# A chunked recurrence with attention behind it: scans and a transpose put behind a mask in VectorE's order

## The chip, the cores and the metric

The kernel runs on one core of a Trainium2 chip. The metric is the device time of one execution in microseconds; the median of several runs is compared. A core has five engines with an instruction queue each: TensorE (PE in the profile), VectorE (DVE), ScalarE (ACT), GpSimd (POOL) and SyncE (SP), which here issues the DMAs. Each takes its instructions in the order in which the program issues them and waits for the others by semaphores.

## The reference

Two stages. The first is a recurrence with a matrix state for each of 4 x 8 heads, over 768 time steps, with 40 x 40 numbers in a state:

```
for t in range(768):
    y[t]  = r[t] @ state
    Sa    = state @ a[t]
    state = state * w[t] - outer(Sa, b[t]) + outer(v[t], k[t])
```

The second takes y as x (4 batches, 768 rows, 320 columns) and computes four attention experts with a causal softmax, of which each row gets its two best by a gate, weighted:

```
for e in range(4):
    ye   = softmax(causal((x @ wq[e]) @ (x @ wk[e]).T / 8)) @ (x @ wv[e]) @ wo[e]
    out += gate[:, e] * ye
```

## The kernel before

The time axis is cut into 24 chunks of 32 steps (NC), and four chunks make a group W of 128 steps (NW = 6 groups). Inside a chunk the recurrence becomes products of small matrices, and the state is handed from chunk to chunk. The work falls into a loop by chunk and a preparation by group.

The loop (MAIN, line 387) runs n from 0 to 24. A step n has ten slots, 0 to 9, and each issues one piece: 0 g of chunk n (products of the state, line 328), 1 f of chunk n-1 (line 342) with its **mask** FX on VectorE (line 343; "F's mask"), 2 t of chunk n-1, 3 u of chunk n (line 333), 4 y of chunk n-1 (lines 353 and 355, 64 products that read FX), 5 z of chunk n-1 (XT, line 357, VectorE), 6 the keys of chunk n+1, 7 s of chunk n (line 373) with the **state update** ST on VectorE (line 380; at a group's last chunk with a gauge, line 364), 8 w of chunk n, 9 v of chunk n+1. The next g reads ST.

The preparation of group W is put into the slots of the steps before it. It is written as strings in SIDE: row r, which holds for step n = 4(W-1) + r, is split at "/", and the k-th part is issued behind the piece of slot k. The first group is prepared in START, and for W=1 rows 0 to 3 come from SIDE1. The letters that the change touches, with a digit ahead of it for one of the two halves of the heads (0 or 1):

- a: suffix products by a scan (line 192, VectorE); b: a reciprocal and a copy (lines 194, 195, VectorE); s: a second scan (line 197, VectorE), which needs a and b.
- X: products with the result of s, two instructions (line 201, GpSimd); K and H: products with the result of a, two instructions each (line 205, GpSimd). Below, the four of K and H of a half are "K pieces", counted from 0K on.
- e: a load; f and g: two range checks (line 189, ScalarE).
- m0, m1: 64 products of a half on TensorE (line 226), for which X, K and H of that half must be done; then the masking of the result (line 229) and its transpose (line 231) on VectorE, and two masked copies on GpSimd (line 233).
- L: the **turning** of the masked products, one transpose of 128 x 1024 (line 242, VectorE), and two clearings (lines 243, 244, GpSimd).
- t and a number: so many of 28 **row operations** (lines 250 and 252, VectorE, in pairs) that invert triangular matrices; the first pair is the shortest and the last too, the middle ones are the longest.
- T: two transposes of the inverse (lines 257, 259, VectorE); B, D: copies on ScalarE (line 265); P, Q: 128 products each (line 272).

Every piece keeps the order of issue of its engine, so a scan in slot 8 stands on VectorE ahead of F's mask of the next step, and a scan in slot 1 behind it.

Of the kernel before, what the change touches and what calls it, by code (L numbers as in the profile page):

```python
# [25 lines left out]
    -3: "//l1///0w///1w",  # L26
    -2: "//l2/////l30f0g/0a0b0s",
    -1: "0X0K0H/1a1b/1e/////1K1H/1f1g1s1X",
    0: "///m0//////m1L",
    1: "/t16//B/////t12",  # L30
    2: "/T////////P",
    3: "///D//////Q",
}

# [1 line left out]
         (1, "0e0l0u1l1u1w1e"), (0, "o0"), (1, "0a0b0K0H"), (0, "i1 L B k0 x3 j47 t28 j0 j23 S o1 Z"), (1, "0f0g1f1g"), (0, "D"), (1, "0s1a0X1H"),  # L36
         (0, "P v0 Q"), (1, "1b1s"))

SIDE1 = ("////////n01p1xi0o0", "///n1i1o1L//Bt6//t8", "/t8//t6////T", "//P/D/////Q")


def layouts(r, k, v, w, a, b):
# [40 lines left out]
def recurrence(tc, ctx, I, xT, FL, CM, early, tail=None):  # L83
# [4 lines left out]
    V, A, T, PL, SY = nc.vector, nc.scalar, nc.tensor, nc.gpsimd, nc.sync  # L88
# [300 lines left out]
    def at(n, s, *fs):  # L389
        jobs.setdefault((n, s), []).extend(fs)  # L390

    def items(W, line, inv, td):

        fs, i = [], 0
        while i < len(line):
            x = line[i]
            if x == " ":
                i += 1
            elif x in "LTSZPQBD":
                fs.append(inv[x])  # L400
                i += 1
            elif x in "tj":
                j = i + 1
                while j < len(line) and line[j].isdigit():
                    j += 1
                m = int(line[i + 1:j])
                if x == "t":
                    fs += td[:m]
                    del td[:m]
                else:  # L410
                    fs.append(lambda m=m: busy(m))
                i = j
            else:
                y = line[i + 1]
                if x == "x":
                    fs.append(lambda y=y: fill(int(y)))
                elif x == "l":
                    fs.append(lambda y=y: load_k(W, int(y)))
                elif x == "c":
                    fs += [lambda k=k, y=y: load_c(int(y), k) for k in (range(4) if y == '0' else (1,))]  # L420
                elif x == "m":
                    fs.append(lambda y=y: mm(W, int(y)))
                elif x in "nio":
                    fs.append(lambda x=x, y=y: mm(W, int(y), x))
                elif x == "v":
                    fs.append(lambda y=y: units[int(y)]["v"]())
                elif x == "k":
                    fs.append(lambda y=y: keys(int(y)))
                else:
                    fs.append(preps[W, int(x)][y])  # L430
                i += 2
        return fs

    preps = {(w, a): prep(w, a) for w in range(NW) for a in range(2)}
    for W in range(1, NW):
        inv = invert(W)
        td = list(inv["t"])
        for r, line in SIDE.items():
            n = 4 * (W - 1) + r
            line = SIDE1[r] if W == 1 and r >= 0 else line  # L440
            for k, part in enumerate(line.split("/") if n >= 0 else ""):
                assert k < 10
                at(n, k, *items(W, part, inv, td))
        assert not td
# [406 lines left out]
def body(tc, I, out):  # L851
    with ExitStack() as ctx:
        dp = ctx.enter_context(tc.tile_pool(name="xd", bufs=1, space=DRAM))
        xT = dp.tile([4, 320, 768], F32, name="xT")
        fp = ctx.enter_context(tc.tile_pool(name="flag", bufs=1))
        FL = fp.tile([128, 24], F32, name="FL")
        CM = fp.tile([128, 261], F32, name="CM")
        FI = fp.tile([1, 1], I32, name="FI")
        with ExitStack() as c1:
            c1.enter_context(tc.manual_schedule())  # L860
            pre = []
            def tail(raw):
                p, jobs = prepare(tc.nc, ctx.enter_context(tc.tile_pool(name="pre", bufs=1, side="right", reuse_waits="tile")), I, xT, raw)
                pre.append(p)
                return jobs
            recurrence(tc, c1, I, xT, FL, CM, ExitStack(), tail)
        with ExitStack() as c2:
            moe(tc, c2, I, xT, out, CM[:, 0:128], pre[0], FL, FI)

        far = tc.nc.values_load(FI, min_val=0, max_val=1)  # L870
        with tc.If(far != 0):
            with ExitStack() as c3:
                c3.enter_context(tc.manual_schedule())
                step_by_step(tc, c3, I["RAW"], xT)
            with ExitStack() as c4:
                moe(tc, c4, I, xT, out, CM[:, 0:128], pre[0])
# [25 lines left out]
```

## Time and profile before

| | |
|---|---|
| runs, us | 609.68, 608.61, 610.55; median 609.68 |
| profiled execution, us | 608.79, its span 607.0 |
| mean granted TensorE clock | 0.986 of full speed |
| busy share of the span | PE 93%, DVE 78%, ACT 60%, POOL 42% |
| chain of work that ended last | PE 60%, DVE 22%, DMA 6%, ACT 5%, issue 3%, POOL 2% |

The chain is followed back from the last instruction of the execution to whatever released each step. Its shares tell which engines set the end over the whole span; what a change in one stretch is worth is read from that stretch.

### The profile page before, as it was taken

How to read it: one execution, taken by the hardware profiler on the slowest of the kernel's cores; microseconds unless marked ns; L12 is line 12 of the kernel's file. 1: busy time of each engine (PE TensorE's matmuls, PEld its weight loads, DVE VectorE, ACT ScalarE, POOL GpSimd, SP SyncE). 2: the span in 40 equal slices, each digit the busy share in tenths (PEclk: the TensorE clock that was granted, in tenths of full speed). 3: DMA queues.
4: the chain of work that ended last, by engine and by line, in shares of the span. 5: the costliest groups of instructions: out<-in, count | busy, mean ns of one | idle time of the engine just before them, and what ended most of it. 6: DMA issues, size and time to landing. Idle time of an engine off the chain costs nothing.

```text
span 607.0 us, 23642 instructions
## 1 busy us (share of the span) xinstructions
PE 566.0 (93%) x10111; PEld 496.1 (82%) x10111; DVE 475.9 (78%) x963; ACT 364.2 (60%) x740; POOL 257.3 (42%) x233
## 2 busy tenths in 40 slices
PE   7998999899999999999999879989999989999996
PEld 3547898899989989989999768878888878987884
DVE  8999899589498678766324369999989997898892
ACT  4854356367356456644546337757776777778873
POOL 5247309807914931960000232546544353333550
PEclk9999999999999999999999879989999999999998
DMA  6622352453354255223146244212311312020102
GB/s 153 176 89 57 119 150 69 119 143 117 94 162 123 78 145 148 67 71 97 49 138 159 55 115 117 53 50 68 84 43 45 82 36 70 24 53 11 56 2 72
DMA packets 44196, 54.09 MB, mean 89 GB/s; under 512 B 20098, under 2 KB 33666, under 8 KB 44082
## 3 DMA queue, kind: packets, MB, share of 16 engines
q1 hardware_dynamic: 43794, 52.32, 31.0%
q8 instruction: 82, 1.34, 0.9%
q10 hardware_dynamic: 288, 0.17, 0.2%
q14 instruction: 32, 0.26, 0.1%
HBM read 38.31 MB, written 7.86 MB: 76 GB/s over the span
## 4 chain that ended last, share of the span: by engine, by line
PE 60%; DVE 22%; DMA 6%; ACT 5%; issue 3%; POOL 2%; SPq 0%; DVEq 0%; ACTq 0%
PE pt L659 6%; PE ot L784 4%; PE pk L272 4%; PE sc L739 4%; PE ps L373 4%; PE pf L353 4%; PE pt L769 4%; PE pt L795 4%; PE pf L355 3%; PE pk L226 3%; PE pg L324 3%; PE pu L333 3%; PE pk L310 3%; PE pg L328 3%; PE pf L342 2%
## 5 line engine op out<-in xcount | busy, mean ns | idle before, releaser
L761 POOL TENSOR_TENSOR P<-P,m 128x128 f32<-128x128 f32 (+2 forms) x96 | 89.1, 950 | 116.5 <-DVE m L757 59.5
L201 POOL TENSOR_TENSOR AB<-EA,SC 40x1024 f32<-40x1024 f32 x18 | 48.9, 2714 | 83.5 <-PE pg L328 61.6
L750 ACT ACTIVATE P<-sc,m 128x128 f32<-128x128 f32 (+2 forms) x96 | 60.8, 634 | 25.5 <-DVE m L749 15.0
L784 PE MATMUL ot<-pt,vv 128*128 128x256 f32 (+1 forms) x384 | 61.1, 292 | 5.7 <-DVE ots L790 5.5
L739 PE MATMUL sc<-ks,qs 128*128 128x384 f32 (+4 forms) x256 | 62.3, 346 | 3.6 <-ACT P L750 2.9
L773 DVE TENSOR_TENSOR pt<-pt,pt 128x384 fp32r<-128x384 f32 (+1 forms) x96 | 59.0, 619 | 5.3 <-ACT pt L772 3.6
L784 PEld LDWEIGHTS ot<-pt,vv 128*128 128x128 f32 x384 | 51.5, 191 | 9.8 <-DVE ots L790 8.2
L749 DVE TENSOR_REDUCE m<-sc 128x1 f32<-128x128 f32 (+2 forms) x96 | 58.7, 615 | 0.9 <-PE sc L742 0.4
L772 ACT ACTIVATE pt<-pt 128x384 fp32r<-128x384 f32 (+1 forms) x96 | 51.9, 543 | 10.5 <-PE pt L769 9.0
L205 POOL TENSOR_TENSOR KB<-KB,SUF 104x512 f32<-104x512 f32 x38 | 57.0, 1534 | 0.9 <-DMA KB<-in_EK 0.5
L769 PE MATMUL pt<-CM,P 128*128 128x128 f32 x336 | 53.0, 275 | 3.8 <-DVE qs L668 2.6
L353 PE MATMUL pf<-FX,LS 128*40 128x64 f32 x768 | 47.7, 224 | 3.6 <-DVE FX L343 3.4
L353 PEld LDWEIGHTS pf<-FX,LS 128*40 128x40 f32 x768 | 42.3, 118 | 6.6 <-DVE FX L343 5.5
L659 PE MATMUL pt<-xh,wq 128*128 128x384 f32 x192 | 42.9, 359 | 4.7 <-DVE qs L668 4.5
L739 PEld LDWEIGHTS sc<-ks,qs 128*128 128x128 f32 x256 | 40.4, 191 | 7.4 <-ACT P L750 6.9
L355 PE MATMUL pf<-RX,SD 80*40 80x64 f32 x736 | 45.8, 222 | 0.0
L233 POOL TENSOR_TENSOR GK<-GK,CM 128x512 f32<-128x512 f32 x23 | 27.5, 1196 | 41.0 <-DVE GK L231 29.8
L335 ACT ACTIVATE R<-pu 32x640 f32<-32x640 f32 x48 | 33.3, 694 | 19.1 <-PE pu L333 18.5
L330 ACT ACTIVATE GT<-pg,CM 128x320 f32<-128x320 f32 x48 | 22.7, 523 | 36.3 <-PE pg L328 36.1
L343 DVE TENSOR_TENSOR FX<-pf,MK 128x1024 f32<-128x1024 f32 x24 | 29.1, 1213 | 18.6 <-PE pf L342 18.5
L769 PEld LDWEIGHTS pt<-CM,P 128*128 128x128 f32 x336 | 36.7, 141 | 7.4 <-issue 3.4
L355 PEld LDWEIGHTS pf<-RX,SD 80*40 80x40 f32 x736 | 41.6, 119 | 0.2 <-ACT SD L350 0.2
(152 smaller groups left out, 1367.4 us busy)
## 6 DMA issues: line engine op xcount, KB each, us to landing
ks<-ks SPq DMA_DIRECT2D x32, 192.0 KB
KB<-in_EK SPq DMA_DIRECT2D x32, 160.0 KB
EA<-in_EA SPq DMA_DIRECT2D x24, 160.0 KB
V<-in_V SPq DMA_DIRECT2D x24, 160.0 KB
R<-in_VX SPq DMA_DIRECT2D x48, 80.0 KB
RX<-in_RX SPq DMA_DIRECT2D x48, 80.0 KB
RB<-in_RB SPq DMA_DIRECT2D x48, 80.0 KB
xT<-XT SPq DMA_DIRECT2D x24, 160.0 KB
```

The lines of the kernel that those rows point to most:

```text
L205: e.tensor_tensor(x, x, sv[:, :, 1:33].rearrange("p (x t c) n -> p x t c n", t=2, c=4)[:, :, t], op=OP.mult)
L353: T.matmul(pf[rows(r), x], ls[:, x, r], FX[:, :, x, r], start=True, stop=c == 0)
L355: T.matmul(pf[rows(r), x], SD[:, x, r], RX[:, :, x, r], start=False, stop=True)
L659: T.matmul(p, w, x, start=(j == 0), stop=(j == len(prs) - 1))
L739: T.matmul(ps[:, c, 0:cw], QS[b][:, e, o], KS[b][:, e, z, k], start=(z == 0), stop=(z == 1 and not last), skip_group_check=True)
L749: V.tensor_reduce(m[:, 0, t:t + 1], ps[:, 0:ch, 0:cw], axis=AX.XY, op=OP.max, negate=True)
L750: later(DE, lambda: A.activation(pv, ps[:, 0:ch, 0:cw], AF.Exp, bias=m[:, 0, t:t + 1], accum_out=m[:, 1, t:t + 1]))
L761: PL.tensor_tensor(P[:, 0:n], P[:, 0:n], m[:, 3, t:t + 1].to_broadcast([128, n]), op=OP.mult)
L769: T.transpose(p[:, 128 * y:128 * y + 128], st["P"][t][:, 128 * c:128 * c + 128], ident)
L772: A.activation(h, p[:, 0:n], AF.Copy)
L773: later(DL, lambda: V.tensor_tensor(l, p[:, 0:n], f32(h), op=OP.subtract))
L784: T.matmul(po[:, 128:256] if one else po, VV[b][:, k, e].rearrange("p a b -> p (a b)"), PT[:, 256 * k:256 * k + (128 if one else 256)], st ...
```

## The change

SIDE1 becomes a dictionary with the same strings. A new SIDE2 holds rows -2, -1 and 0 of the third group (W=2, steps 2, 3 and 4). Rows 0 to 2 of SIDE change for the groups W=2 to 5.

```diff
-    0: "///m0//////m1L",
-    1: "/t16//B/////t12",
-    2: "/T////////P",
+    0: "///m0//////m1",
+    1: "/Lt14//B/////t12",
+    2: "/t2T////////P",
...
+SIDE2 = {-2: "//l2/////l30f0g", -1: "/0a0b0s0X0K0H1a1b/1e//////1f1g/1K1H", 0: "/1s1X//m0//////m1"}
...
-            line = SIDE1[r] if W == 1 and r >= 0 else line
+            line = {1: SIDE1, 2: SIDE2}.get(W, {}).get(r, line)
```

By step and slot, for the third group:

| | before | after |
|---|---|---|
| 0a 0b 0s | step 2, slot 8 | step 3, slot 1 |
| 0X 0K 0H | step 3, slot 0 | step 3, slot 1 |
| 1a 1b | step 3, slot 1 | step 3, slot 1 |
| 1K 1H | step 3, slot 7 | step 3, slot 9 |
| 1f 1g | step 3, slot 8 | step 3, slot 8 |
| 1s 1X | step 3, slot 8 | step 4, slot 1 |
| m0, m1 | step 4, slots 3, 9 | step 4, slots 3, 9 |

For each group W=2 to 5, with n = 4(W-1): L goes from step n, slot 9 to step n+1, slot 1, behind F's mask; of the 28 row operations 14 in place of 16 follow in that slot, 12 in slot 8 as before, and the last 2 in step n+2, slot 1, ahead of T.

## Rows read from the trace of the kernel before

**Rows 1.** Page: span of the profiled execution.

```profile
span 607.0 us, 23642 instructions
```

**Rows 2.** Chain of waits, third group: start us, length us, what.

```profile
99.51 5.80 POOL KB L205 x4
```

**Rows 3.** VectorE's timeline: start us, us, engine, line, operation, tiles, shapes, count [idle before].

```profile
86.28 2.30 DVE L192 TENSOR_TENSOR_SCAN SUF<-EW,D 104x1056 f32<-104x1056 f32 x1
...
88.86 2.36 DVE L197 TENSOR_TENSOR_SCAN SC<-EW,D1P 104x1056 f32<-104x1056 f32 x1
91.13 1.20 DVE L343 TENSOR_TENSOR FX<-pf,MK 128x1024 f32<-128x1024 f32 x1
92.25 3.48 DVE L192 TENSOR_TENSOR_SCAN SUF<-EW,D 104x1056 f32<-104x1056 f32 x1
```

**Rows 4.** GpSimd's timeline, third group.

```profile
91.35 2.16 POOL L201 TENSOR_TENSOR AB<-EA,SC 40x1024 f32<-40x1024 f32 x1 [18.84 <-DMA EA<-in_EA]
93.58 4.11 POOL L201 TENSOR_TENSOR AB<-EA,SC 40x1024 f32<-40x1024 f32 x1
97.77 1.74 POOL L205 TENSOR_TENSOR KB<-KB,SUF 104x512 f32<-104x512 f32 x1
...
102.93 3.24 POOL L205 TENSOR_TENSOR KB<-KB,SUF 104x512 f32<-104x512 f32 x1
107.28 2.33 POOL L205 TENSOR_TENSOR KB<-KB,SUF 104x512 f32<-104x512 f32 x2
```

**Rows 5.** TensorE's timeline: f of chunk 2, m1, f and y of two chunks.

```profile
85.54 1.15 PE L342 MATMUL pf<-RB,VR 80*64 80x64 f32 x32 [0.17 <-ACT VR L339]
...
114.03 2.09 PE L226 MATMUL pk<-KB,AB 104*64 104x64 f32 x64 [1.24 <-POOL AB L201]
...
116.85 1.13 PE L342 MATMUL pf<-RB,VR 80*64 80x64 f32 x32
...
120.60 0.36 PE L353 MATMUL pf<-FX,LS 128*40 128x64 f32 x3 [0.55 <-DVE FX L343]
...
130.58 0.36 PE L353 MATMUL pf<-FX,LS 128*40 128x64 f32 x3
```

**Rows 6.** VectorE's timeline behind m1: L, F's mask, row operations, the next mask.

```profile
117.47 1.96 DVE L242 STREAM_TRANSPOSE MT<-GB 128x1024 f32<-128x1024 f32 x1
119.37 1.18 DVE L343 TENSOR_TENSOR FX<-pf,MK 128x1024 f32<-128x1024 f32 x1
120.47 0.17 DVE L250 TENSOR_TENSOR TP<-MT 128x28 f32<-128x28 f32 x1
...
124.32 0.28 DVE L250 TENSOR_TENSOR TP<-MT 128x112 f32<-128x112 f32 x1
124.63 0.28 DVE L252 TENSOR_TENSOR MT<-MT,TP 128x112 f32<-128x112 f32 x1
...
128.70 0.21 DVE L252 TENSOR_TENSOR MT<-MT,TP 128x52 f32<-128x52 f32 x1
...
129.19 0.21 DVE L252 TENSOR_TENSOR MT<-MT,TP 128x28 f32<-128x28 f32 x1
129.31 1.22 DVE L343 TENSOR_TENSOR FX<-pf,MK 128x1024 f32<-128x1024 f32 x1
```

**Rows 7.** VectorE's timeline, first group: L with a row operation directly behind.

```profile
31.22 2.00 DVE L242 STREAM_TRANSPOSE MT<-GB 128x1024 f32<-128x1024 f32 x1
33.26 0.19 DVE L250 TENSOR_TENSOR TP<-MT 128x28 f32<-128x28 f32 x1
```

**Rows 8.** Windows: from:to us, length, each engine's busy us (instructions), PEclk, DMA, GB/s.

```profile
120.65:122.65 2.00, 2.00 (x65) 1.92 (x65) 1.74 (x8) 1.95 (x4) 0.00 (x0) 1.00 0.25 98
342.00:344.00 2.00, 2.00 (x44) 2.00 (x40) 0.00 (x0) 0.00 (x0) 0.00 (x0) 0.50 0.04 8
352.00:354.00 2.00, 0.00 (x0) 0.00 (x0) 0.30 (x1) 0.10 (x2) 0.00 (x0) 1.00 0.89 266
356.00:358.00 2.00, 2.00 (x7) 2.00 (x8) 2.00 (x14) 0.00 (x0) 1.42 (x2) 0.50 0.10 25
```

More of the change, by code (lines that the diff above doesn't have):

```diff
@@ L37 @@
          (0, "P v0 Q"), (1, "1b1s"))
-SIDE1 = ("////////n01p1xi0o0", "///n1i1o1L//Bt6//t8", "/t8//t6////T", "//P/D/////Q")
+SIDE1 = {0: "////////n01p1xi0o0", 1: "///n1i1o1L//Bt6//t8", 2: "/t8//t6////T", 3: "//P/D/////Q"}
+SIDE2 = {-2: "//l2/////l30f0g", -1: "/0a0b0s0X0K0H1a1b/1e//////1f1g/1K1H", 0: "/1s1X//m0//////m1"}
 def layouts(r, k, v, w, a, b):
```

## The prediction

> **What bounds the kernel now.** I read the page first, then the chain of waits, then the engines' timelines around the two places that the diff touches. The span is 607.0 us [rows 1]; the profiled execution took 608.79 us, so 1.8 us lie around it, and nothing of the change is there. The recurrence fills somewhat over half of the span, and in most of it TensorE follows itself without a gap: whatever delays one of its products delays all behind it. Two kinds of place break that, and both are in the diff.
>
> The first is the third group (W=2). There the chain runs over GpSimd [rows 2]: from 91.35 us, when the scan 0s has ended, until just ahead of 114.03 GpSimd works without a pause through 0X, 0K, 0H, 1K, 1H and 1X, and the products m1 start at 114.03, after TensorE stood idle for 1.24 us [rows 3, 5]. Products that follow m1 in TensorE's order are held too. So the end depends there on when 0s ends and on how long GpSimd takes from then.
>
> The second comes in each of the groups W=2 to 5, right after m1: VectorE is busy without a pause from the masking of m1's result to F's mask of the next step [rows 6], and TensorE waits for it twice, 0.55 us ahead of y at 120.60 and next to nothing at 130.58, where the mask ends at 129.31 + 1.22 = 130.53 [rows 5, 6]. The four groups repeat this within 0.03 us.
>
> **Part 1: the third group's scans behind F's masks.** Same instructions, other places. In step 2 VectorE comes to 0a at 86.28 and to F's mask of chunk 2 only at 91.13, though f's last product ended at 85.54 + 1.15 = 86.69 [rows 3, 5]. After the change the mask starts at about 86.7, and the next instruction 1.12 later (91.13 to 92.25) at 87.82. 0a then starts 1.54 us later than before, 0s ends at 88.86 + 2.36 + 1.54 = 92.76, and 0X, which needs 0s and began 0.13 after its end, starts at 92.9 in place of 91.35: +1.54.
>
> What TensorE gains by the earlier mask, whose y it can begin sooner, is worth nothing: it then waits longer for GpSimd at m1.
>
> GpSimd's run from there is 22.6 us, of which 4.6 is stretching: the second half of 0X takes 4.11 against 2.16 for the first (+1.95), the first of the K pieces 1.74 and the fifth 3.24 against 2.33/2 = 1.17 (+0.57, +2.07) [rows 4]. The first of these fits the scan 1a: 1a is issued at 92.25 while 0X's first half runs until 93.51, ends at 95.73 (3.48 us where 0a takes 2.30 [rows 3]), and 0X's second half ends 2 us behind that. So each waits for the other's whole instruction. After the change 1a is issued right behind 0s, where the mask stood before: 87.82 + 4.85 (86.28 to 91.13) = 92.7, just ahead of 0X. If it holds GpSimd for all of its 2.30 us, 0X's first half waits from 92.9 to 95.0, 2.1 us; the gauge of the state then costs GpSimd 0.6 to 0.7 as before, and 1s up to 2.3 in place of 2.07. Stretching becomes 4.7 to 5.1. I take +0.45, so m1 starts at 114.03 + 1.54 + 0.45 = 116.0: **+2.0 us**. The low end is -1.24, since TensorE itself is ready for m1 no earlier than 112.8 and all of the stretching would have to go; if the stretching stays as it is, it is +1.54; the high end is +2.1, when 1s too holds GpSimd for its whole length.
>
> Which of the two goes first when a scan is issued 0.2 us ahead of GpSimd's instruction, the rows on 1a do not show; there GpSimd was first [rows 4]. The Trainium skill (SBUF — State Buffer, section "SBUF: two separate sides") says that VectorE with two inputs in SBUF and GpSimd reading SBUF take the shared port pair as an exclusive lock for a whole instruction, whoever starts first. By that rule the sum is the 2.0 us; with the order of before kept, it would be 1.54.
>
> The other moves of part 1 add nothing. 1K and 1H go from slot 7 to slot 9 of step 3, but GpSimd, which takes its work in order, gets to them only behind 0H, at 102.93 before and later now. 1X goes to slot 1 of step 4, behind 1s as before; GpSimd gets to it only behind 1H. ScalarE's 1f and 1g keep their slot, no DMA moves, and SP's queue keeps its order. 0a, 0s and 1a now stand between F's mask and the XT and state updates of step 3, but the time until the gauge is the same work in another order; what is late there ends ahead of m1's wait.
>
> **Part 2: the turning L behind F's mask, t16/t12 into t14/t12/t2 (four groups).** Before, L starts at 117.47, the mask at 119.37, the first row operation at 120.47 [rows 6]. After, the mask waits for f, which ends at 116.85 + 1.13 = 117.98 [rows 5]: it starts at 118.0, which leaves VectorE idle for 0.5 us. L follows 1.10 us behind (the mask's own pitch, 119.37 to 120.47). The first row operation now stands directly behind L and reads what L writes; the trace has that once, in the first group, 31.22 to 33.26, 2.04 us [rows 7], against 1.90 where the mask lay between. So it starts at 118.0 + 1.10 + 2.04 = 121.14, 0.67 later. The two row operations that leave this stretch give back 2 x 0.31 = 0.62 (124.32 to 124.63): XT and the state update come 0.05 later. In slot 8 those two come in (+0.62) and the two shortest leave; the mask follows 0.12 behind the last operation (129.19 to 129.31), so without them it would follow the one at 128.70 at 128.82 and gain 0.49. Sum at the next mask: 0.05 + 0.62 - 0.49 = +0.18 us. TensorE's y waits for that mask, so 0.18 is late there, though its wait of 0.55 ahead of the y before is gone: that gain ends at the state update, for which the next g has to wait. What moves behind this mask (t2, about 0.46) is hidden by the wait of the next state update for TensorE. GpSimd's two clearings behind L stand off this path.
>
> Times four: **+0.7 us**. The ends: -2.2, if all of 0.55 per group stays gained; +1.2, if the mask's start behind f and the reading behind L each cost another 0.06. I take the sum from the rows.
>
> **Sum.** 2.0 + 0.7 = +2.7 us. On the profiled execution that is 608.79 + 2.7 = 611.5. The median of the runs shown (609.68) lies 0.9 above that execution, and a median of new runs will be compared with it: 612.4 us.
>
> **Rivals.**
> B. The turning pays: VectorE is not what sets the second mask, and 0.55 us per group is gained, -2.2, beside +2.0 of part 1: 609.5. For it: TensorE does wait there. Against: VectorE has no idle time from 117.47 to the mask at 129.31 [rows 6]. Chance 0.13.
> C. GpSimd is not slower but quicker, the end on the other side: the 4.6 us of stretching go, because the scans no longer meet 0X and the K pieces. Then m1 starts when TensorE is ready, -1.24, and with +0.7 it is -0.5: 609.1, not slower. It decides from the point where the stretching falls below 4.6 - 1.54 = 3.1 us. For it: 1a starts ahead of 0X. Against: ahead or behind, its time is added once, and 1s still meets the K pieces. Chance 0.12.
> D. TensorE's clock falls in the longer wait. The trace has a stretch with TensorE idle (352 to 354) after which the granted clock is 0.50, the lower of its levels, 1.2 GHz, and one where it ran 44 products in 2 us at 0.50 against 65 in 2 us at 1.00 [rows 8]; y's 64 products would take 2.9 in place of 2.0, +0.9: 613.3. The Trainium skill (TensorE: Matmul & The Clock Gate, section "HAM oscillation — how this bites in real kernels") has idle gaps between groups of products lowering the clock. Against: the 1.24 us wait of today does not do it, and the longer one (some 3.3 to 4 us) is likely split between m0 and m1, which both wait for GpSimd. Chance 0.17.
> E. The change does not take effect, since what holds VectorE is something that both orders share; both parts cost nothing: 609.7. Chance 0.08.
>
> **How the numbers follow.** The forecast has 0.50 and alone would span 611.2 to 613.3. About 0.3%, 1.8 us, is what a measurement of this kernel can tell from no change; the line lies at 611.5. Slower: 0.45 of the forecast and D, 0.62. Faster by over 0.3% needs B and C at once or C with more: 0.05. Within: 0.33. The range takes in D and B and leaves most of C out: 609.2 to 614.0.
>
> **What would show it.** In the changed profile, F's mask of step 3 starts 4.4 us earlier (by about 86.7), 0X starts 1.5 us later, at 92.9, GpSimd's run to the end of 1X takes 22.6 to 23.1 us, and the idle time of TensorE ahead of m0 and m1 together rises from 1.24 to 3.3 or more. In each of the four groups VectorE idles 0.5 us ahead of the mask, L follows it, y directly behind has no wait and the next y starts about 0.2 us later than before, counted from m1. I am wrong if 0X's halves and the K pieces run at 2.16 and 1.17 throughout, if m1 starts earlier than 114 us, or if the time from m1 to the second y shrinks.

## The result and the profile after

The changed kernel takes 614.51 us (median of 6 runs, 612.26 to 615.22), the one before 609.22 (6 runs, 608.26 to 610.55): a ratio of 1.0092, with a 95% interval of 1.0070 to 1.0115. It is slower by 5.3 us by the medians (5.6 by the ratio) where 2.7 were forecast, and 614.5 lies above the range's upper end of 614.0. The profiled execution of after took 614.90 us, 6.1 more than that of before. In the changed kernel every line number behind the strings is higher by 2.

The page of after answers to [rows 1] with:

```profile
span 613.1 us, 23645 instructions
```

VectorE's timeline of after in step 3 (columns as in [rows 3]): F's mask comes first, then 0a, 0s and 1a.

```profile
86.68 1.23 DVE L345 TENSOR_TENSOR FX<-pf,MK 128x1024 f32<-128x1024 f32 x1 [0.28 <-PE pf L344]
87.82 2.35 DVE L194 TENSOR_TENSOR_SCAN SUF<-EW,D 104x1056 f32<-104x1056 f32 x1
...
90.45 2.36 DVE L199 TENSOR_TENSOR_SCAN SC<-EW,D1P 104x1056 f32<-104x1056 f32 x1
92.72 2.33 DVE L194 TENSOR_TENSOR_SCAN SUF<-EW,D 104x1056 f32<-104x1056 f32 x1
```

The mask is 4.45 us earlier, at 86.68 in place of 91.13, and 0s ends at 92.81. 1a, at 92.72, is undisturbed: 2.33 us, where it took 3.48 in [rows 3]. GpSimd's timeline of after, the two halves of 0X, the K pieces as one group, and 1X (columns as in [rows 4]; the second fence is VectorE's 1s):

```profile
92.94 4.08 POOL L203 TENSOR_TENSOR AB<-EA,SC 40x1024 f32<-40x1024 f32 x1 [20.46 <-DMA EA<-in_EA]
97.10 2.73 POOL L203 TENSOR_TENSOR AB<-EA,SC 40x1024 f32<-40x1024 f32 x1
99.91 11.29 POOL L207 TENSOR_TENSOR KB<-KB,SUF 104x512 f32<-104x512 f32 x8
111.15 4.40 POOL L203 TENSOR_TENSOR AB<-EA,SC 40x1024 f32<-40x1024 f32 x2
```

```profile
103.98 2.79 DVE L199 TENSOR_TENSOR_SCAN SC<-EW,D1P 104x1056 f32<-104x1056 f32 x1
```

0X starts 1.59 us later than in [rows 4]. Now its first half is the stretched one (4.08), the second is so by 0.57 (2.73 against 2.16). From 92.94 to the end of 1X at 115.55 GpSimd takes 22.6 us, as before. TensorE's timeline of after, from m0 to the second y behind m1 (columns as in [rows 5]):

```profile
104.79 2.08 PE L228 MATMUL pk<-KB,AB 104*64 104x64 f32 x64
...
115.60 3.68 PE L228 MATMUL pk<-KB,AB 104*64 104x64 f32 x64 [3.15 <-POOL AB L203]
119.07 1.88 PE L330 MATMUL pg<-ST,AB 104*64 104x40 f32 x32
120.74 1.95 PE L344 MATMUL pf<-RB,VR 80*64 80x64 f32 x32
122.63 1.61 PE L351 MATMUL ps<-CM,ST 104*80 104x104 f32 x8
124.17 2.35 PE L335 MATMUL pu<-GT,TT 64*32 64x80 f32 x32
...
136.69 0.32 PE L355 MATMUL pf<-FX,LS 128*40 128x64 f32 x4
```

m1 starts 1.57 us later than in [rows 5], after 3.15 us of waiting in place of 1.24. New is its length: 3.68 us in place of 2.09, and all behind it is longer in the same way (f 1.95 against 1.13; g 1.88 against 1.08, in the row of before here).

```profile
115.95 1.08 PE L328 MATMUL pg<-ST,AB 104*64 104x40 f32 x32
```

The windows of after show why (columns as in [rows 8]):

```profile
112.00:113.00 1.00, 0.45 (x16) 0.33 (x12) 0.00 (x0) 0.48 (x1) 1.00 (x1) 1.00 0.82 162
113.00:114.00 1.00, 0.00 (x0) 0.00 (x0) 0.00 (x0) 0.00 (x0) 0.93 (x2) 0.90 0.46 147
114.00:115.00 1.00, 0.00 (x0) 0.00 (x0) 0.00 (x0) 0.00 (x0) 1.00 (x1) 0.50 0.62 199
...
116.00:120.00 4.00, 4.00 (x81) 4.00 (x79) 0.60 (x1) 0.00 (x0) 1.81 (x2) 0.50 0.07 23
120.00:124.00 4.00, 4.00 (x58) 3.76 (x56) 1.97 (x4) 0.94 (x2) 2.19 (x2) 0.50 0.08 17
124.00:128.00 4.00, 4.00 (x72) 3.61 (x72) 3.69 (x10) 2.06 (x3) 0.46 (x2) 0.57 0.36 112
128.00:132.00 4.00, 4.00 (x106) 3.60 (x100) 2.93 (x9) 2.32 (x5) 0.00 (x0) 1.00 0.27 76
```

With TensorE idle from 112.45 (the 0.45 us busy in the first row), the granted clock falls to 0.50, 1.2 GHz, at about 113.8 (0.90 over the microsecond from 113, which begins at 1.00), and is back at 1.00, 2.4 GHz, at about 127.4: 0.57 over four us leaves 3.4 of them at 0.50. That is some 13.6 us at the lower level, of which most is work. Before, the clock is 1.00 in each window of 4 us from 104 to 132.

In the next three groups it stays up. The fourth one's m1 and second y, and VectorE between them:

```profile
169.60 2.08 PE L228 MATMUL pk<-KB,AB 104*64 104x64 f32 x64
...
186.43 0.36 PE L355 MATMUL pf<-FX,LS 128*40 128x64 f32 x3 [0.28 <-DVE FX L345]
```

```profile
173.60 1.23 DVE L345 TENSOR_TENSOR FX<-pf,MK 128x1024 f32<-128x1024 f32 x1 [0.48 <-PE pf L344]
174.74 2.00 DVE L244 STREAM_TRANSPOSE MT<-GB 128x1024 f32<-128x1024 f32 x1
176.77 0.19 DVE L252 TENSOR_TENSOR TP<-MT 128x28 f32<-128x28 f32 x1
...
185.16 1.22 DVE L345 TENSOR_TENSOR FX<-pf,MK 128x1024 f32<-128x1024 f32 x1
```

From m1 to the second y it is 16.83 us (16.83, 16.82 and 16.84 in the three groups); before it was 16.55 to 16.58 [rows 5]. In the third group it is 136.69 - 115.60 = 21.09.

So the 6.1 us of the two profiled executions divide: 1.57 at the third group's m1; 21.09 - 16.83 = 4.26 behind it at the lower clock; 4 x 0.25 = 1.0 in the groups. That is 6.8. At the recurrence's last mask the difference is 346.20 - 339.50 = 6.70. Behind it the execution of before has a stretch at the lower clock ([rows 8], 342 to 344) that after's does not have, so that the last y took 1.3 us longer there; the difference is 5.37 at the last XT. The 0.7 up to the 6.1 of the end arise in the second stage, which the diff does not touch, and were not traced further.

### The profile page after: what moved, and what is told of

The parts are those of the page before. It is cut to its first block, busy times and chain, and to the rows that moved or that the text cites. A ratio compares the mean times of both kernels' runs of the same rounds, so it can differ in the third digit from the quotient of the medians.

```text
span 613.1 us, 23645 instructions
## 1 busy us (share of the span) xinstructions
PE 568.8 (93%) x10111; PEld 499.0 (81%) x10111; DVE 475.7 (78%) x963; ACT 364.1 (59%) x740; POOL 257.5 (42%) x233
## 4 chain that ended last, share of the span: by engine, by line
PE 58%; DVE 23%; DMA 6%; ACT 5%; issue 4%; POOL 2%; SPq 1%; DVEq 0%; ACTq 0%
PE pk L274 5%; PE pt L661 5%; PE ot L786 4%; PE pu L335 4%; PE sc L741 4%; PE ps L375 3%; PE pf L355 3%; PE pt L771 3%; PE pk L228 3%; PE pf L344 3%; PE pg L330 3%; PE pt L797 3%; PE pg L326 3%; PE pf L357 3%; DVE m L751 3%
## 5 line engine op out<-in xcount | busy, mean ns | idle before, releaser
L355 PE MATMUL pf<-FX,LS 128*40 128x64 f32 x768 | 46.3, 222 | 1.3 <-DVE FX L345 1.3
L357 PE MATMUL pf<-RX,SD 80*40 80x64 f32 x736 | 44.5, 219 | 0.1
L355 PEld LDWEIGHTS pf<-FX,LS 128*40 128x40 f32 x768 | 39.8, 116 | 4.0 <-DVE FX L345 2.1
L357 PEld LDWEIGHTS pf<-RX,SD 80*40 80x40 f32 x736 | 39.1, 117 | 0.2 <-ACT SD L352 0.2
```

The costliest lines, as they stand in the source:

```text
L355: T.matmul(pf[rows(r), x], ls[:, x, r], FX[:, :, x, r], start=True, stop=c == 0)
L357: T.matmul(pf[rows(r), x], SD[:, x, r], RX[:, :, x, r], start=False, stop=True)
```

## The experiments

The theory after the result: the wait of 3.15 us in one piece lets the clock fall, and the work done at half clock is over half of the loss. Rivals: part 2 costs more than its rows say; or the third group's new order itself delays work behind m1. The first four kernels were timed against 29 runs of before on one chip (median 608.02), the last three against 29 on another (median 607.9); after's own ratio, 1.0092, is against the six runs named above. Differences in us are worked out from the ratios. Where SIDE2 is there, the rows carry after's line numbers (those of the long wait three more), else those of before.

**Part 1 alone.** The third group has after's scans, the turning stays ahead of the mask everywhere.

```diff
+SIDE2 = {-2: "//l2/////l30f0g", -1: "/0a0b0s0X0K0H1a1b/1e//////1f1g/1K1H", 0: "/1s1X//m0//////m1L"}
...
-            line = SIDE1[r] if W == 1 and r >= 0 else line
+            line = SIDE1[r] if W == 1 and r >= 0 else SIDE2.get(r, line) if W == 2 else line
```

> Part 1 alone: the third group's scans moved, the turning and the row operations as before. Theory 1 (the clock): GpSimd starts 0X about 1.5 us later, TensorE waits some 3 us ahead of m1 of the third group, its granted clock falls to 0.50 for over 10 us behind that wait, and the kernel is 4 to 5 us slower than before (1.6 from GpSimd's later start, the rest from the clock). Theory 2 (the moves themselves, no part for the clock): 1.5 to 2 us slower, and the rest of the loss lies in part 2.

Measured: 612.60 us (12 runs), ratio 1.0077 (1.0053 to 1.0101): +4.7 us for a part that was to cost 2.0. TensorE's m1 and the windows around it, in this trace:

```profile
116.82 3.59 PE L228 MATMUL pk<-KB,AB 104*64 104x64 f32 x64 [3.40 <-POOL AB L203]
```

```profile
116.00:117.00 1.00, 0.18 (x4) 0.18 (x6) 0.00 (x0) 0.00 (x0) 0.92 (x2) 0.88 0.70 200
...
120.00:121.00 1.00, 1.00 (x38) 1.00 (x34) 0.47 (x1) 0.00 (x0) 0.00 (x0) 0.91 0.00 0
```

The clock falls here too, at about 116.8, but is back at about 120.2: 3.4 us where over 10 were expected, and from m1 to the second mask it is 16.79 us against 15.28 before, +1.5. (The whole trace stands 1.2 us later than after's by the time of 0X, 94.15 against 92.94, with a stretch at the lower clock from 55 to 59 us that after's does not have.) This profiled execution took 611.90; the twelve go from 608.19 to 614.92, far wider than after's six, and their mean granted clocks from 0.976 to 0.990. So the length of the lower clock is not the same from trace to trace, and the median of these runs most likely holds a mixture. Part 1 carries most of the loss, and it carries the fall of the clock.

**Part 2 alone.** The rows 0 to 2 of the change, the third group's scans as before.

```diff
-    0: "///m0//////m1L",
-    1: "/t16//B/////t12",
-    2: "/T////////P",
+    0: "///m0//////m1",
+    1: "/Lt14//B/////t12",
+    2: "/t2T////////P",
```

> Part 2 alone: the turning behind F's mask and the 14, 12 and 2 row operations in the groups W=2 to 5, the scans as before. Theory 1: m1 to the second y behind it takes 16.8 us in place of 16.6 in each of the four groups, the clock in the recurrence stays at 1.00, the kernel is 1.0 us slower (0.2%). Theory 2: 3 us or more slower.

Measured: 609.34 us (12 runs), ratio 1.0025 (1.0003 to 1.0048), +1.5 us with an interval of 0.2 to 2.9. The masks behind m1, which starts at 115.22 after a wait of 1.28, and TensorE's g of the step between them:

```profile
119.22 1.22 DVE L343 TENSOR_TENSOR FX<-pf,MK 128x1024 f32<-128x1024 f32 x1 [0.48 <-PE pf L342]
...
130.78 1.22 DVE L343 TENSOR_TENSOR FX<-pf,MK 128x1024 f32<-128x1024 f32 x1
```

```profile
127.62 1.13 PE L328 MATMUL pg<-ST,AB 104*64 104x40 f32 x32 [0.67 <-DVE ST L380]
```

From m1 to the second mask it is 15.56 us, 0.28 more than the 15.28 of [rows 5, 6], with the clock at 1.00 in every window from 112 to 136. The first y comes 5.95 us behind m1, 0.62 earlier than before, but that is lost again: TensorE now waits 0.67 us for the state update ahead of the next g, where it did not wait before. (This execution, 606.33, is the fastest of the twelve; the 0.28 is counted from m1 within it.) So part 2 is slower by itself, also where no clock falls, by some 1 us over four groups: the rival that makes it the main loss falls. The interval is too wide to tell 1.0 from the predicted 0.7.

**The wait filled.** The changed kernel, with twelve products of 128 columns by 512 in bf16 on TensorE ahead of m1; nobody reads their result.

```diff
-SIDE2 = {-2: "//l2/////l30f0g", -1: "/0a0b0s0X0K0H1a1b/1e//////1f1g/1K1H", 0: "/1s1X//m0//////m1"}
+SIDE2 = {-2: "//l2/////l30f0g", -1: "/0a0b0s0X0K0H1a1b/1e//////1f1g/1K1H", 0: "/1s1X//m0//////j12m1"}
```

> The changed kernel with 12 more products of TensorE, some 2.6 us, right ahead of m1 of the third group; they use a finished buffer, and the output is the same. m1 itself still waits for GpSimd until about 115.6 us. Theory 1: the granted clock stays at 1.00 behind m1, m1 to the second y takes 16.8 us in place of 21.1, and of the loss some 2.6 us are left (1.6 + 4 x 0.25). Theory 2: the time stays at that of the changed kernel, 5 us slower than before.

Measured: 609.68 us (13 runs), ratio 1.0036 (1.0015 to 1.0057), +2.2 us. The two pieces of TensorE's timeline, VectorE's second mask and the windows:

```profile
113.76 2.76 PE L174 MATMUL pf<-D 104*128 104x512 bf16 x12
117.21 2.08 PE L228 MATMUL pk<-KB,AB 104*64 104x64 f32 x64 [0.69 <-POOL AB L203]
```

```profile
132.78 1.22 DVE L345 TENSOR_TENSOR FX<-pf,MK 128x1024 f32<-128x1024 f32 x1
```

```profile
112.00:116.00 4.00, 4.00 (x65) 2.58 (x61) 0.82 (x1) 1.02 (x1) 3.92 (x3) 1.00 0.70 177
116.00:120.00 4.00, 3.31 (x99) 2.81 (x97) 0.58 (x1) 0.00 (x0) 3.36 (x3) 1.00 0.26 72
```

Work that is worth nothing makes the kernel faster (1.0036 against 1.0092, with intervals that do not meet): m1 starts no earlier (0X starts at 94.52 here, 1.58 later than after's, and m1 1.61 later), but it takes 2.08 us again, and the second mask is 15.57 behind it in place of after's 135.20 - 115.60 = 19.60. (This execution, 613.48, is the slowest of the thirteen; it is 1.6 us behind after's ahead of m1 already, and its clock falls once more at the recurrence's end, where after's does not.) What is left, 2.2 us, is near the two terms that do not depend on the clock, 1.57 + 1.0 = 2.6. This tells the theory from the rival of the new order: the order is unchanged here.

**A long wait in the old order.** The kernel before; in the third group GpSimd does the first instruction of 1X twice, with the same result. SIDE2 is read as in part 1 alone, here and in the kernels below that have it.

```diff
+SIDE2 = {-1: "0X0K0H/1a1b/1e/////1K1H/1f1g1s1J1X"}
...
+        def again():
+            x = ab[rows(0), :, 0:32]
+            PL.tensor_tensor(x, ea[rows(0)], sc[rows(0), :, 0:32], op=OP.mult)
-        return dict(w=load_w, e=load_a, l=lambda: load_k(0), u=lambda: load_k(1),
+        return dict(J=again, w=load_w, e=load_a, l=lambda: load_k(0), u=lambda: load_k(1),
```

> The kernel before, in its old order; only GpSimd does the first instruction of the third group's 1X twice, 2.2 us more work with the same result. TensorE's wait ahead of m1 grows from 1.24 to about 3.4 us. Theory 1: the granted clock falls as in the changed kernel, and the kernel is 5 to 6.5 us slower (2.2 from the wait, the rest from the clock). Theory 2: 2.2 us slower.

Measured: 613.49 us (6 runs), ratio 1.0098 (1.0070 to 1.0127), +6.0 us, for 2.2 us added on GpSimd. m1 and four windows:

```profile
116.99 3.68 PE L231 MATMUL pk<-KB,AB 104*64 104x64 f32 x64 [3.52 <-POOL AB L203]
```

```profile
116.00:120.00 4.00, 3.01 (x56) 3.01 (x58) 0.00 (x0) 0.00 (x0) 3.12 (x3) 0.52 0.24 65
120.00:124.00 4.00, 4.00 (x78) 3.90 (x74) 3.19 (x3) 0.94 (x2) 1.74 (x2) 0.50 0.01 4
...
128.00:132.00 4.00, 4.00 (x84) 3.79 (x84) 2.24 (x7) 3.04 (x5) 0.00 (x0) 0.77 0.06 15
```

The clock is down for 3.8 + 4 + 4 + 1.8 = 13.7 us, and the second mask comes 136.91 - 116.99 = 19.92 us behind m1. Neither the scans nor the turning were touched. A longer wait alone brings a loss of after's size.

**1X taken off GpSimd.** The kernel before, with the third group's 1X done on VectorE, to take away the wait ahead of m1 altogether.

```diff
+SIDE2 = {-1: "0X0K0H/1a1b/1e/////1K1H/1f1g1s", 0: "/1x//m0//////m1L"}
```

> The kernel before with one thing moved: the third group's 1X (4.4 us on GpSimd) is done by VectorE, behind F's mask of step 4. Theory 1 (GpSimd's run sets when m1 of the third group starts): GpSimd is done with 1H by about 112 us, TensorE's wait ahead of m1 goes from 1.24 to under 0.5 us, and the kernel is about 1 us faster (0.2%). Rival: VectorE's two products hold GpSimd up and delay F's mask's followers as much as they save, no change.

Measured: 611.95 us (12 runs), ratio 1.0056 (1.0029 to 1.0084), +3.4 us where a gain was expected. In VectorE's, TensorE's and the windows' rows of this trace:

```profile
107.62 4.17 DVE L203 TENSOR_TENSOR AB<-EA,SC 40x1024 f32<-40x1024 f32 x2
```

```profile
113.18 1.44 PE L312 MATMUL pk<-CM,KB 104*128 104x104 f32 x8 [2.85 <-DVE GK L233]
...
118.47 2.09 PE L228 MATMUL pk<-KB,AB 104*64 104x64 f32 x64
```

```profile
113.00:114.00 1.00, 0.82 (x6) 0.82 (x7) 0.70 (x2) 0.00 (x0) 0.80 (x1) 0.73 0.00 0
...
116.00:117.00 1.00, 1.00 (x20) 0.79 (x18) 0.00 (x0) 0.00 (x0) 0.00 (x0) 0.57 0.75 150
```

m1 waits for nothing now. But the two instructions take 4.17 us on VectorE beside GpSimd's K pieces, and m0's masking and transpose, queued behind them, start at 111.81 and 112.42. The keys wait 2.85 us for that transpose, and the clock falls at the end of their wait, for 3.4 us (113.5 to 116.9). The wait was not removed but moved to a place 5 us earlier in TensorE's order.

**Fewer row operations ahead of the mask.** The kernel before, with the turning behind the mask as in part 2, but split 10, 12 and 6: the 26 row operations ahead of the second mask become 22.

```diff
-    0: "///m0//////m1L",
-    1: "/t16//B/////t12",
-    2: "/T////////P",
+    0: "///m0//////m1",
+    1: "/Lt10//B/////t12",
+    2: "/t6T////////P",
```

> The turning behind F's mask as in the change, the scans as before, but the 28 row operations split 10, 12 and 6 in place of 14, 12 and 2. Theory 1 (the turning costs 0.25 us a group because VectorE's work ahead of the second mask grew): with four more operations behind that mask, the second y behind m1 comes 16.0 us after m1 in place of 16.6 before and 16.8 in the change, and the kernel is about 2 us faster than before (0.35%). Rival (the cost is the order itself): 16.8 and 1 us slower than before.

Measured: 604.84 us (12 runs), ratio 0.9941 (0.9917 to 0.9964): faster than both kernels, by 3.6 us against before. The masks behind m1 at 114.85, and the second y:

```profile
118.85 1.23 DVE L343 TENSOR_TENSOR FX<-pf,MK 128x1024 f32<-128x1024 f32 x1 [0.48 <-PE pf L342]
...
129.38 1.22 DVE L343 TENSOR_TENSOR FX<-pf,MK 128x1024 f32<-128x1024 f32 x1
```

```profile
130.65 0.36 PE L353 MATMUL pf<-FX,LS 128*40 128x64 f32 x3
```

From m1 to the second mask it is 14.53 us: 1.03 less than with 14, 12 and 2, which is four operations at a pitch of some 0.26, and 0.75 less than before. That y has next to no wait left: the mask ends at 129.38 + 1.22 = 130.60, and TensorE is busy until then. The first y comes 5.95 us behind m1, as in part 2 alone, but here the next g does not wait for the state update: it starts 11.66 us behind m1 (126.51), in place of 12.40 with 14, 12 and 2 and 12.35 before. So the 0.55 us a group that rival B hoped for is kept only where fewer row operations stand ahead of the state update. Whether the split would win as much with the turning ahead of the mask was not run. Of the 0.75, 0.41 is left at the next m1 (164.07 - 114.85 = 49.22, before 49.63), since that m1 now waits for GpSimd:

```profile
164.07 2.08 PE L226 MATMUL pk<-KB,AB 104*64 104x64 f32 x64 [0.37 <-POOL AB L201]
```

To the last mask, 338.09, the four groups together have won 2.2 us. What the measured 3.6 (2.2 to 5.0) may hold beyond that stays open; the execution of before had its 1.3 us of lower clock at the recurrence's end, this one had not.

**Both.** 1X on VectorE with the split 10, 12 and 6.

```diff
+SIDE2 = {-1: "0X0K0H/1a1b/1e/////1K1H/1f1g1s", 0: "/1x//m0//////m1"}
...
+    0: "///m0//////m1",
+    1: "/Lt10//B/////t12",
+    2: "/t6T////////P",
```

> Both together: the third group's 1X on VectorE behind F's mask, and the turning behind F's mask with row operations split 10, 12 and 6. Theory 1: the two gains add, about 3 us faster than before (0.5%), the clock at 1.00 in the recurrence. Rival: the two meet on VectorE and give no more than one of them.

Measured: 608.89 us (12 runs), ratio 1.0002 (0.9979 to 1.0024). TensorE's row and two windows:

```profile
111.98 1.65 PE L312 MATMUL pk<-CM,KB 104*128 104x104 f32 x8 [2.85 <-DVE GK L233]
```

```profile
111.00:112.00 1.00, 0.02 (x1) 0.02 (x1) 1.00 (x3) 0.00 (x0) 0.65 (x1) 0.50 0.00 0
...
114.00:118.00 4.00, 4.00 (x70) 3.63 (x68) 0.82 (x1) 1.37 (x2) 0.27 (x1) 0.52 0.59 142
```

The 3 us that were expected did not come, since 1X on VectorE is a loss. The keys' wait is that of the kernel with 1X on VectorE, and the clock falls in it again, here for 6.8 us (111.0 to 117.8) in place of 3.4. Together they cost 3.7 us against the split alone (1.0002 - 0.9941), as 1X on VectorE cost 3.4 against before. The two effects, a loss and a gain, add within their intervals, and the split alone stays the best of these kernels.

## Why the direction was right and the time wrong

**Right: the direction, and where it comes from.** Slower was the likeliest case, and both parts are slower alone.

**Part 1, the start of 0X: right.** The mask was put at 86.7 (86.68), 0a at 87.82 (87.82), 0X at 92.9 (92.94).

**Part 1, GpSimd's stretching: below what I took.** I took +0.45, though the terms named there (2.1, 0.6 to 0.7, and 2.07 as before) make only 0.2 to 0.3 over the 4.6, and 0.45 had 1s near its full length; the run took 22.6 us as before and m1 came 1.57 later, where "if the stretching stays as it is, it is +1.54". 1a did go ahead of 0X and held its first half (1.92 us), as assumed. Each of the three terms came out a little under what I took: 1a 1.92 (2.1), 0X's second half 0.57 (0.6 to 0.7), and the eight K pieces beside 1s 11.29 - 8 x 1.17 = 1.9 (up to 2.3). The rule weighed there holds by these rows: the Trainium skill (SBUF — State Buffer, section "SBUF: two separate sides") has whoever starts first hold the shared ports for a whole instruction, and 1a, ahead by 0.2 us, ran 2.33 us undisturbed while 0X's first half took 4.08 in place of 2.16.

**Part 2: right, a little small.** 0.25 us a group at the second y against 0.18 (0.28 at the second mask). The mask comes 4.00 us behind m1 (3.97 predicted), L 1.14 behind it (1.10), the first row operation 2.03 behind L (2.04): the first two are 0.07 of what is missing. VectorE idles 0.48 ahead of the mask (0.5). The y behind the mask has no wait, and what it gains is given back at the state update, as the prediction said: 0.67 us of wait ahead of g.

**Wrong: the clock, in its chance and in its price.** The sum, 2.0 + 0.7, has no term for the clock. The prediction had it as rival D at 0.17 and +0.9 us, and both numbers failed.
- The chance rested on two points. That a wait of 1.24 us does not do it held. The other, "the longer one (some 3.3 to 4 us) is likely split between m0 and m1, which both wait for GpSimd", failed: m0 waited for nothing: 104.79 directly behind u. The trace of before had said so (its u and m0 stand below the list): m0 ran there at 105.13, again directly behind u, and the fifth K piece, the first that m0 does not need, began at 102.93 [rows 4]. m0's inputs were ready 2.2 us ahead of it, more than the 2.0 that they would be late by the forecast. All of the delay had to go into the wait of m1, which rose from 1.24 to 3.15 us in one piece; the 3.3 or more that the prediction named as a sign was missed by little.
- The price was that of y's 64 products. The clock fell inside the wait, and m1, g, f, t and u were all slow before y came: m1 +1.59, g +0.80, f +0.82, each by the rows of after against those of before. F's mask comes 122.74 - 115.60 = 7.14 us behind m1 in place of 4.00, the second mask another 0.90 later, and the second y 0.22: +4.26 in this execution. These are the products on the path, and a stretch at 0.50 is charged with all of them. The Trainium skill (TensorE: Matmul & The Clock Gate, section "HAM oscillation — how this bites in real kernels") has a wait make the next group of products start at the low clock; the trace agrees, with m1 at 3.68 us in place of 2.09 and g, f, t and u behind it.

```profile
103.90 1.30 PE L333 MATMUL pu<-GT,TT 64*32 64x80 f32 x32
105.13 2.08 PE L226 MATMUL pk<-KB,AB 104*64 104x64 f32 x64
```

The sum by measured terms, for the profiled executions: 1.57 + 1.0 + 4.26 = 6.8, of which 6.1 reached the end. By the ratios it is 5.6 without and 2.2 with the wait filled, so the clock is some 3.4 of it.

**What stays open.** How long the lower clock lasts: it was 3.4 us in the trace of part 1 alone and 13.6 and 13.7 us in those of after and of the long wait, for waits of 3.40, 3.15 and 3.52 us. Behind the same wait of 2.85 us, ahead of the same keys, it was 3.4 us in the trace of 1X on VectorE and 6.8 in that of both. So the length of the wait alone does not decide it, and what does was not found. Nor did the clock fall at the same point of the wait: some 1.35 us into it in after, 2.7 in the long wait, and at its very end in part 1 alone. By the length of the lower clock alone, the loss behind m1 differs between the traces of after and of part 1 alone by 4.26 - 1.51 = 2.75 us.

## What to carry to other kernels

When a change lengthens a wait of TensorE, find out first whether the wait comes in one piece (the slack of each product that waits for the same engine says so), and then price it with the clock's fall: every product on the path behind it at the lower level's duration, here for 3.4 to 13.7 us, not the wait alone. An instruction that was moved behind a mask paid here only where the work left ahead of the next state update and mask shrank with it: 14, 12 and 2 lost where 10, 12 and 6 won. Taking an instruction off the engine that is waited for is worth nothing where it delays the work of the engine that takes it over, and an earlier wait needs that work.

## What was not expected of the hardware

- Ahead of m1 a wait of 1.24 to 1.28 us left the clock at 1.00; waits of 2.85, 3.15, 3.40 and 3.52 us were each followed by a stretch at 0.50. The wait is not all of it: at the recurrence's end the clock of before fell at about 340.6, in the second of two waits of 1.18 and 0.49 us. Within half a microsecond of the same y it fell in the traces of the wait filled, of 1X on VectorE and of both too, and not in those of after and of the other four.
- In after the clock stayed at 0.50 for some 12 us in which TensorE worked without a gap (115.60 to 127.4).
- Products that nobody needs, 2.76 us of them, put into a wait, saved 3.4 us by the ratios.
